# Strided and local attention before two gated products: prologue loads cut in 15/16 and 1/16 of their rows, wider query-key matmuls, small matmuls ahead

## The chip, the cores and the metric

One core of a Trainium2 chip runs the kernel. The metric is the device time of one execution in microseconds (us), as the median of several runs. Beside it one execution was taken by the hardware profiler; its rows are those quoted here. Engines are named as in the profile: PE (TensorE's matmuls), PEld (its weight loads), DVE (VectorE), ACT (ScalarE), POOL (GpSimd), SP (SyncE, which issues the transfers).

## The reference

The inputs are q, k, v of 4 batches x 8 heads x 576 positions x 64, and three weight matrices for each of two gated products on 2304 tokens of 512.

```
scores = scale * np.matmul(q, k.transpose(0, 1, 3, 2))
mask_local = (rel >= 0) & (rel < stride)                  # heads 0 to 3, stride 32
mask_strided = (rel >= 0) & (pos[None, :] % stride == pos[:, None] % stride)   # heads 4 to 7
...
attn = np.exp(scores - max);  attn = attn / (sum + 1e-09);  x = np.matmul(attn, v)
x = (x @ w_a) * (x @ w_b) @ w_out
x = sigmoid(x @ w_gate) * (x @ w_val) @ w_out
```

## The kernel before

The 576 positions are cut into tiles of 128 (the last has 64), and a tile of all four batches makes 512 tokens. The first tile is the prologue: its attention has to be done before the first gated product has anything to multiply. From there on the products of a tile run on PE while DVE and ACT do the attention of the next tile and convert the weights.

**The local heads of the first tile** are four groups, one per batch (`attention`, with `first` true). A group is a chain over the engines: load of q and k (`load_qk`) and of v for two batches at a time (`load_v`); on PE the mask by a matmul with the identity and then eight matmuls of 64 rows by 64 keys (`qk`, L605 and L611); on DVE maximum (L623); on ACT four exponentials (L629); the sum's reciprocal (L635, L636) and the normalisation (`normalise`, L644) on whichever of POOL, DVE and ACT the plan finds free first; four transposes on PE (L652), a copy on ACT (L658), the product with v on PE (L668), and two parts of the result on ACT and DVE (L677, L680), which are columns of the tiles x12 and x14. The strided heads of the same tile are `strided_first` (scores L994 and L1001, transposes L1032, values L1065, results L1082 and L1086 in x13 and x15).

**The weights** come in pieces of 512 KB (`convert`). Each is turned from its stored form on ACT (L519), DVE (L528), ACT (L536) and DVE (L540). The first three go to the buffer `raw`. The next three (`k == 1`) go to a place of their own in w4, and before each of these loads POOL copies one element from the landed first weight into that place (L512), so that the load waits for it.

**The order** on each engine is made by a planner (`Plan.run`): it keeps a time for each engine, takes the operation that can begin first, and writes the engines' streams in that order. The times are costs given with each operation, such as 450 for a load on SP or 1050 for a normalisation on POOL. Nothing of it is known to the chip: there each engine takes its stream in order and waits at semaphores. Where the planner leaves a gap on PE in the first 27 us, it fills it with matmuls by zeros (`plan.fill`, L447, and L1056 later on).

The products of the first tile with w_a and w_b are L1117, with w_out L1208; the second gated product is L1489.

Of the kernel before, what the change touches and what calls it, by code (L numbers as in the profile page):

```python
# [11 lines left out]
U16 = mybir.dt.uint16  # L12
# [45 lines left out]

IDLE_BANK, FILL_TO = 3, 27e3
FILL = (430, 8e3, 225)  # L60

M1, M2 = 400, 50

# [119 lines left out]
class Plan:  # L183
# [85 lines left out]

    def run(self):  # L270
        avail = dict.fromkeys(("PE", "ACT", "DVE", "POOL", "SP", "ACTQ"), 0.0)
        dma = 0.0
        left = {}
        after = {}
        ready = []
        for op in self.ops:
            left[op] = len(op.deps)
            for d in op.deps:
                after.setdefault(d, []).append(op)
            if not op.deps:  # L280
                ready.append(op)
        while ready:
            best = None
            for op in ready:
                s = self.start(op, avail)
                if s is None:
                    continue
                t, eng, cost, slots = s
                rank = (max(t, avail[eng]), op.key, op.seq)
                if best is None or rank < best[0]:  # L290
                    best = rank, op, eng, cost, slots
            if best is None:
                raise RuntimeError("no operation can be issued")
            rank, op, eng, cost, slots = best
            ready.remove(op)
            if eng == "PE" and self.fill and rank[0] < FILL_TO:
                t = avail["PE"]
                while True:
                    t += FILL[0] if t < FILL[1] else FILL[2]
                    if t > rank[0]:  # L300
                        break
                    self.fill()
            op.eng = eng
            op.slot = {}
            for (ring, _), (_, s) in slots.items():
                op.slot.setdefault(ring, []).append(s)
                self.held[ring, s] = op
            op.end = avail[eng] = rank[0] + cost
            if op.size:
                early = eng == "SP" and op.end < 20e3  # L310
                dma = max(dma, op.end + 700) + op.size / (330 if early else 350)

                op.end = dma + (1700 if early else 1200)
            op.fn(op)
            for ring, owner in op.free:
                if isinstance(owner, tuple):
                    held = owner[0].slot[ring][owner[1]:owner[1] + 1]
                else:
                    held = owner.slot[ring]
                for s in held:  # L320
                    del self.held[ring, s]
                    self.since[ring, s] = op.end
            for x in after.get(op, ()):
                left[x] -= 1
                if not left[x]:
                    ready.append(x)
        self.makespan = max(avail.values())
# [35 lines left out]
def attention_moe_kernel(ctx, tc, qkv, fqk, fvv, fq, fk, fv, sq, sk, sv, w1, w2, mask, ident, out):  # L363
# [77 lines left out]
    for n in range(B):  # L441
# [5 lines left out]
    plan.fill = lambda: PE.matmul(  # L447
        idle, nil, nil.unsqueeze(1).to_broadcast([P, 4, P]), start=True, stop=True)

    c_id = add("ACTQ", 600, lambda op: ACT.dma_start(out=idt, in_=ident), size=1 << 16)  # L450
    mask_at = weight(2, KF - 7, 1, EARLY)

# [31 lines left out]
    def convert(w, need, start=()):  # L484
        parts, done, merges = {}, {}, []
        tops, firsts = [], []

        def clear(op):
            for i in op.slot["c"]:
                tops.append(at(PLACE["c"] + i * DM, DM, FIRST, U32))  # L490
                POOL.memset(tops[-1], 0)

        c_top = add("POOL", 1000, clear, start, key=need(0, 0) - AHEAD - 10,
                    take=[("c", F_RING[:1]), ("c", F_RING[1:])])
        for c in range(3 * KF):
            k, m = divmod(c, 3)
            x = {}
            key = need(k, m) - AHEAD
            at_load = key - LEAD

            if k == 0 and m < 2:
                key -= EARLIER

            own = (RAW_ZONE * ZONE + m * 2 * DM, 2 * DM, EARLY) if k == 1 else None
            if k == 0:
                firsts.append(x)

            def load(op, x=x, k=k, m=m, own=own):

                x["raw"] = at(*own, U32) if own else raw(op, U32)[:, :2 * DM]  # L510
                if own:
                    POOL.tensor_copy(out=x["raw"][:1, :1], in_=firsts[m]["raw"][:1, 1:2])  # L512
                nc.sync.dma_start(
                    out=x["raw"].bitcast(U16)[:, :4 * DM - 1], in_=w[k, m].bitcast(U16)[:, 1:]
                )

            def top(op, x=x):
                x["t"] = tops[op.slot[f"t{id(w)}"][0]]
                ACT.activation(  # L519
                    out=x["t"].bitcast(F16).rearrange("p (n two) -> p n two", two=2)[:, :, 1],  # L520
                    in_=x["raw"].bitcast(BF16).rearrange("p (n four) -> p n four", four=4)[:, :, 2],
                    func=AF.Copy, scale=0.5,
                )

            def merge(op, x=x):
                u = x["raw"].rearrange("p (n two) -> p n two", two=2)[:, :, 0]
                x["f"] = u.bitcast(F32)
                DVE.scalar_tensor_tensor(  # L528
                    out=u, in0=u, scalar=13, in1=x["t"],
                    op0=ALU.logical_shift_right, op1=ALU.bitwise_or,  # L530
                )

            def high_part(op, x=x, k=k, m=m):
                hi, lo = (at(*weight(m, k, i), F32R) for i in range(2))
                parts[m, k] = hi, lo
                ACT.activation(out=hi, in_=x["f"], func=AF.Copy, scale=256.0)  # L536

            def low_part(op, x=x, k=k, m=m):
                hi, lo = parts[m, k]
                DVE.scalar_tensor_tensor(  # L540
                    out=lo, in0=x["f"], scalar=256.0, in1=r32(hi),
                    op0=ALU.mult, op1=ALU.subtract,
                )

            plan.slack = M2
            taken = [] if own else [("raw", (0, 1, 2))]
            used = [own] if own else []
            after = [firsts[m]["op"]] if own else []
            a = touch(add("SP", 450, load, list(start) + after, key=at_load, take=taken, size=1 << 19), (), used)
            x["op"] = a  # L550
            b = touch(add("ACT", act(512), top, [a, c_top], key, take=[(f"t{id(w)}", (0, 1))]), used)
            end = c == 3 * KF - 1
            f = add("DVE", dve(512), merge, [b] + merges * end, key,
                    free=[(f"t{id(w)}", b)] + [("c", c_top)] * end)
            merges.append(f)
            touch(f, (), used)
            g = touch(add("ACT", act(512), high_part, [f], key), used, [weight(m, k, 0)])
            h = touch(add("DVE", dve(512), low_part, [g], key, free=[] if own else [("raw", a)]), used, [weight(m, k, 1)])
            done[m, k] = g, h
            plan.slack = 0  # L560
        return parts, done
# [5 lines left out]
    def attention(g, key, banks, first, war, load=(), held=None, last=True):  # L567
# [13 lines left out]
        def load_qk(op):  # L581
            if first:
                a = at(*eqk)[:, :QW + KW]
                nc.sync.dma_start(out=a, in_=fqk[n])
                x["q"], x["k"] = a[:, :QW], a[:, QW:]
            else:
                a = qk_buf(op)[:, :QW + g.kw]
# [2 lines left out]

        def load_v(op):
            if first:
                nc.sync.dma_start(out=at(*evv)[:WB], in_=fvv[:, n // 2 * 2 * VW:][:, :2 * VW])
                return
            x["v"] = small(op)[:WB, :g.vw]
            nc.sync.dma_start(out=x["v"], in_=qkv[n, :WB, QW + KW:QW + KW + g.vw])
# [5 lines left out]
        def qk(op):  # L602
# [3 lines left out]
            e = at(*ee) if first else small(op)  # L606
            x["e"] = e[:, :g.width]
            for i in range(g.nb):
                for e in range(2):
                    o, k = i * WB + e * HB, g.key(i) + e * HB  # L610
                    PE.matmul(  # L611
# [79 lines left out]
        def ring(*r):  # L691
# [2 lines left out]

        qks, vs, es = ((0, 1), V_RING[:2], E_RING) if g.i != 1 else ((0,), V_RING[:1], E_RING[:1])

        lq = add("SP", 450, load_qk, load, key=FRONT_KEYS[0][n] if first else key - 10, take=ring(("qk", qks)),
                 size=P * (QW + g.kw) * 4)
        used(lq, (), [eqk])
        if first and n % 2:  # L700
            lv = pairs[n // 2]
        else:
            lv = add("SP", 450, load_v, load, key=FRONT_KEYS[1][n // 2] if first else key - 8, take=ring(("c", vs)),
                     size=WB * g.vw * 4 * (1 + first))
            used(lv, (), [evv])
            if first:
# [260 lines left out]
    def strided_first(key):  # L967
# [8 lines left out]
        qa, ka, va, ea, pa = FRONTS["strided"]  # L976

        def load(a, src, at_key):
            return touch(add("SP", 450, lambda op: nc.sync.dma_start(out=at(*a), in_=src), (), at_key,
                             size=P * a[1] * 4), (), [a])  # L980

        lq, lk, lv = (load(a, b, c) for a, b, c in zip((qa, ka, va), (fq, fk, fv), FRONT_KEYS[2]))
# [822 lines left out]
```

## Time and profile before

| | |
|---|---|
| median of 3 runs | 901.54 us (901.32 to 901.73) |
| the profiled execution | 900.82 us |
| its span, first to last instruction | 899.0 us |
| PE busy | 889.7 us (99%) |
| DVE, ACT, POOL busy | 647.4, 405.3, 3.6 us |
| mean granted PE clock | 0.998 |

The busy share of PE is near the whole span, so the time is that of PE's work and of the few places where it waits. A timeline shows for each piece the start, the duration, the engine and line, what it writes and reads, and in brackets how long the engine had been idle before it and what released it; "issue" is a wait that nothing in the profile explains. The queue called instruction in the tables of transfers brings the engines' programs; q8 moves packets of 16 KB.

### The profile page before, as it was taken

The page shows a single profiled execution, that of the slowest core. Times are in us where ns is not written, and L with a number is a line of the kernel's source. Part 1 is how long each engine was busy: PE and PEld are TensorE (multiplying, and loading weights), DVE is VectorE, ACT ScalarE, POOL GpSimd, SP SyncE. Part 2 cuts the span into 40 slices and gives each one's busy share as a digit, 9 for nine tenths or more (in the row PEclk, how much of TensorE's full clock was granted, in tenths as well). Part 3 has the DMA queues.
Part 4 walks back from the last instruction along what each step waited for, and adds up shares of the span by engine and source line. Part 5 has one row for each costly group of instructions (what it writes and reads, how often), then busy time and mean ns, then how long its engine had stood idle before and what let it go on. Part 6 is the DMA issues. An engine that isn't in the chain of part 4 may idle for free.

```text
span 899.0 us, 14095 instructions
## 1 busy us (share of the span) xinstructions
PE 889.7 (99%) x5408; PEld 801.9 (89%) x5408; DVE 647.4 (72%) x1062; ACT 405.3 (45%) x841; POOL 3.6 (0%) x15
## 2 busy tenths in 40 slices
PE   8999999999999999999999999999999999999998
PEld 4788888888888888888899999999999999999998
DVE  4999988998999779811329876674768468649491
ACT  4876644411242113311236655564656545435351
POOL 0000000000000000000000000000000000000000
PEclk9999999999999999999999999999999999999999
DMA  8676664212332123300035243645675598953501
GB/s 306 226 252 191 197 207 131 92 44 63 89 131 72 54 65 117 124 1 0 1 118 164 94 141 127 201 157 186 213 230 181 183 325 317 375 166 116 168 18 61
DMA packets 60515, 132.72 MB, mean 148 GB/s; under 512 B 5728, under 2 KB 35040, under 8 KB 59552
## 3 DMA queue, kind: packets, MB, share of 16 engines
q1 hardware_dynamic: 60160, 131.60, 44.2%
q8 instruction: 42, 0.69, 0.3%
q10 hardware_dynamic: 288, 0.23, 0.1%
q14 instruction: 25, 0.20, 0.1%
HBM read 97.20 MB, written 34.60 MB: 147 GB/s over the span
## 4 chain that ended last, share of the span: by engine, by line
PE 98%; DVE 1%; ACT 1%; issue 0%
PE bank L1489 43%; PE bank L1117 33%; PE bank L1208 17%; PE bank L668 1%; PE bank L611 1%; PE bank L652 1%; PE idle L447 1%; PE bank L938 0%; ACT w8p L629 0%; DVE w4p L1445 0%; PE bank L1065 0%; DVE rest L1501 0%; ACT w4p L1442 0%; PE bank L1056 0%; DVE rest L1572 0%
## 5 line engine op out<-in xcount | busy, mean ns | idle before, releaser
L1142 ACT CAST h16p<-rest 128x512 fp32r<-128x512 f32 (+1 forms) x60 | 34.7, 579 | 133.2 <-PE bank L1208 132.5
L1501 DVE TENSOR_TENSOR rest<-bank,rest 128x384 f32<-128x384 f32 x84 | 46.3, 554 | 57.8 <-PE bank L1489 32.4
L1138 DVE TENSOR_TENSOR rest<-bank,rest 128x512 f32<-128x512 f32 (+1 forms) x60 | 38.1, 634 | 52.0 <-PE bank L1117 51.1
L1262 ACT COPY rest<-bank 128x512 f32<-128x512 f32 (+1 forms) x60 | 32.6, 544 | 91.1 <-PE bank L1117 89.2
L1507 ACT COPY rest<-bank 128x384 f32<-128x384 f32 x84 | 40.2, 479 | 66.1 <-PE bank L1489 65.9
L1146 DVE TENSOR_TENSOR h16p<-rest,h16p 128x512 fp32r<-128x512 f32 (+1 forms) x60 | 38.1, 635 | 29.9 <-PE bank L1208 23.2
L842 DVE TENSOR_TENSOR rest<-rest 128x320 f32<-128x320 f32 (+13 forms) x56 | 51.5, 920 | 1.5 <-DMA rest<-sq 0.5
L905 DVE TENSOR_TENSOR rest<-rest,s 128x320 f32<-128x320 f32 (+13 forms) x56 | 51.5, 919 | 0.9
L912 DVE TENSOR_REDUCE rest<-rest 128x64 f32<-128x320 f32 (+13 forms) x56 | 51.2, 914 | 1.0
L848 DVE TENSOR_REDUCE s<-rest 128x5 f32<-128x320 f32 (+13 forms) x56 | 51.1, 913 | 1.0
L1399 DVE SCALAR_TENSOR_TENSOR rest<-rest 128x512 uint32<-128x512 uint32 x36 | 24.6, 687 | 11.8 <-ACT rest L1392 11.6
L1392 ACT ACTIVATE rest<-rest 128x512 f16<-128x512 bf16 x36 | 28.0, 790 | 7.4 <-DMA rest<-w 7.4
L519 ACT ACTIVATE rest<-rest 128x512 f16<-128x512 bf16 x33 | 26.2, 795 | 10.0 <-DMA rest<-w 9.7
L1572 DVE TENSOR_TENSOR rest<-bank,rest 128x384 f32<-128x384 f32 x36 | 20.0, 556 | 12.4 <-PE bank L1489 10.6
L1566 ACT ACTIVATE rest<-bank 128x384 f32<-128x384 f32 x36 | 17.6, 490 | 22.3 <-PE bank L1489 22.0
L1511 ACT COPY bank<-bank 128x384 f32<-128x384 f32 x42 | 19.5, 466 | 17.3 <-PE bank L1489 16.9
L629 ACT ACTIVATE rest<-bank,nm 128x96 f32<-128x96 f32 x56 | 18.3, 338 | 12.0 <-DVE nm L624 10.5
L528 DVE SCALAR_TENSOR_TENSOR rest<-rest 128x512 uint32<-128x512 uint32 x33 | 22.5, 684 | 0.4 <-ACT rest L519 0.2
L1566 ACT ACTIVATE rest<-rest 128x768 f32<-128x768 f32 x18 | 15.3, 848 | 13.9 <-DVE rest L1501 13.6
L1489 PE MATMUL bank<-w8p,w10p 128*128 128x384 f32 x100 | 20.7, 334 | 0.0
L1489 PEld LDWEIGHTS bank<-w8p,w10p 128*128 128x128 f32 x100 | 17.6, 188 | 0.0
L1489 PE MATMUL bank<-x15p,w3p 128*128 128x384 f32 x88 | 17.5, 334 | 0.0
(494 smaller groups left out, 2395.9 us busy)
## 6 DMA issues: line engine op xcount, KB each, us to landing
rest<-w SPq DMA_DIRECT2D x69, 511.8 KB, 4.3
h2d<-rest SPq DMA_DIRECT2D x18, 768.0 KB, 4.0
rest<-qkv SPq DMA_DIRECT2D x12, 416.0 KB, 4.3
w2p<-h2d SPq DMA_DIRECT2D x12, 384.0 KB, 5.5
w0p<-h2d SPq DMA_DIRECT2D x12, 384.0 KB, 5.2
w1p<-h2d SPq DMA_DIRECT2D x12, 384.0 KB, 5.8
out<-rest SPq DMA_DIRECT2D x24, 192.0 KB, 1.8
x2d<-rest SPq DMA_DIRECT2D x16, 256.0 KB, 2.5
```

The lines of the kernel that those rows point to most:

```text
L842: engine[op.eng].tensor_tensor(out=product(op, n), in0=x["k", h][:, :, :n, :], in1=x["q"][h // 2][:, e:e + nh, j:j + 1, :].to_broadcast([P ...
L848: DVE.tensor_reduce(out=weights_of(h, j, n), in_=x["p", op.deps[0]], op=ALU.add, axis=AX.X)
L905: engine[op.eng].tensor_tensor(out=product(op, n, "p (h d t) -> p h d t"), in0=x["v", h][:, :, :, :n], in1=weights_of(h, j, n).unsqueeze(2 ...
L912: DVE.tensor_reduce(out=xs[:, j, e:e + nh, :], in_=x["p", op.deps[0]], op=ALU.add, axis=AX.X)
L1117: PE.matmul(x[tag][:, :n], ww[:, c * P:(c + 1) * P], xx(c), start=(u == 0 and c == chunks[0]), stop=(u == last and c == chunks[-1]),)
L1138: DVE.tensor_tensor(out=x["g"], in0=x["b"][:, :n], in1=x["g"], op=ALU.mult)
L1142: ACT.copy(out=x["hh"], in_=x["g"])
L1146: DVE.tensor_tensor(out=x["hl"], in0=x["g"], in1=r32(x["hh"]), op=ALU.subtract)
L1208: PE.matmul(ps[:, :n], ww[:, m * P:(m + 1) * P], x[xx], start=start, stop=stop)
L1489: PE.matmul(bank_of(where), at(*lhs(a, (0, 1, 0)[q], c), F32R), at(*rhs(b, (0, 0, 1)[q], c), F32R), start=p in OPENS and (q, c) == units[0 ...
L1501: DVE.tensor_tensor(out=at(*o), in0=bank_of("Z"), in1=at(*a), op=ALU.add)
L1507: "ACT", act2(NS), lambda op: ACT.copy(out=at(*o), in_=bank_of("Y")), [ops[after]], key - 20))
```

## The change

There are three edits. `split_load` replaces the transfers of the prologue: the rows of each are cut in a first piece of 15/16 (120 of 128, or 90 of 96) and a second one of 1/16, which are issued one behind the other. This holds for q, k and v of the first tile, for the strided heads' q, k and v, and for the first six weight loads (`w is w1 and k < 2`). The planner's cost of these loads goes from 450 to 900. The query-key matmuls of the first tile take 128 rows by 96 keys, so that a group has four of them where it had eight; what is computed beside the masked band is masked before. Eighteen matmuls of 32 x 32 zeros stand ahead of everything on PE, at 30 each in the plan.

```diff
+PADS = 18
...
         avail = dict.fromkeys(("PE", "ACT", "DVE", "POOL", "SP", "ACTQ"), 0.0)
+        avail["PE"] = 30.0 * PADS
...
+    for _ in range(PADS):
+        PE.matmul(idle[:32, :32], nil[:32, :32], nil[:32, :32], start=True, stop=True)
+
+    def split_load(out, src):
+        n = out.shape[0] // 16 * 15
+        nc.sync.dma_start(out=out[:n], in_=src[:n])
+        nc.sync.dma_start(out=out[n:], in_=src[n:])
...
-                nc.sync.dma_start(
-                    out=x["raw"].bitcast(U16)[:, :4 * DM - 1], in_=w[k, m].bitcast(U16)[:, 1:]
+                (split_load if w is w1 and k < 2 else nc.sync.dma_start)(
+                    x["raw"].bitcast(U16)[:, :4 * DM - 1], w[k, m].bitcast(U16)[:, 1:]
                 )
...
-            a = touch(add("SP", 450, load, list(start) + after, key=at_load, take=taken, size=1 << 19), (), used)
+            a = touch(add("SP", 450 + 450 * (w is w1 and k < 2), load, list(start) + after, key=at_load, take=taken, size=1 << 19), (), used)
...
-                nc.sync.dma_start(out=a, in_=fqk[n])
+                split_load(a, fqk[n])
...
             for i in range(g.nb):
+                if first:
+                    PE.matmul(g.shaped(x["s"])[:, i // 2, i % 2], x["q"][:, i * P:(i + 1) * P],
+                              x["k"][:, g.key(i):g.key(i) + WB],
+                              start=False, stop=i == g.nb - 1, skip_group_check=True)
+                    continue
```

Since costs in the plan change, the planner writes other orders. Lines of the changed kernel are 10 to 15 higher than those of the same code before (L652 becomes L667).

**POOL**, from its first memsets on (w4p is the place of the weights with k == 1, w7p the scores of batches 2 and 3, nm_293 the sums of batch 3). Before:

```order
L491 MEMSET rest 128x512 x2
L512 COPY w4p_80<-rest 1x1 x3
L793 MEMSET s_474 128x128
L793 MEMSET s_1384 128x192
L793 MEMSET s_2028 128x256
```

And in the changed kernel:

```order
L501 MEMSET rest 128x512 x2
L522 COPY w4p_80<-rest 1x1
L659 ISA
L659 TENSOR_TENSOR w7p_83<-w7p_83,nm_293 128x384
L522 COPY w4p_80<-rest 1x1 x2
L808 MEMSET s_491 128x128
```

The normalisation of batch 3 has moved from DVE to POOL, between the first and the second of the copies that release weight loads. The instruction called ISA ahead of it is new as well: in the built program it is a reload of GpSimd's library 0, put directly ahead of the operation; the program before has none.

**PE**, at the transposes of batch 1 (bank_273 before, bank_266 now). Before:

```order
L652 MATMUL bank_238<-idt,w8p_84 96x128 x4
L605 LDWEIGHTS idb
L605 MATMUL bank_246<-mskb,idb 128x384
L611 MATMUL bank_246<-w9p_85 64x64 x8
L605 LDWEIGHTS idb
L605 MATMUL bank_258<-mskb,idb 128x384
L611 MATMUL bank_258<-w9p_85 64x64 x8
L652 MATMUL bank_273<-idt,w8p_84 96x128 x4
L447 LDWEIGHTS nil
L447 MATMUL idle<-nil 128x512
```

And in the changed kernel:

```order
L667 MATMUL bank_266<-idt,w8p_84 96x128 x4
L615 LDWEIGHTS idb
L615 MATMUL bank_274<-mskb,idb 128x384
L620 MATMUL bank_274<-w9p_85 128x96 x4
L615 LDWEIGHTS idb
L615 MATMUL bank_283<-mskb,idb 128x384
L620 MATMUL bank_283<-w9p_85 128x96 x4
L449 LDWEIGHTS nil
L449 MATMUL idle<-nil 128x512
```

The transposes of batch 1 now stand ahead of the scores of batches 2 and 3, and those of batch 0 have gone ahead of the strided scores. Counted in the built programs (an f32 matmul is four instructions, a transpose two, the others one), instruction 450 of PE is the second of the transposes of batch 1 before, and is among the first products with v (L683) now.

**PE**, at the transposes of batch 3 (bank_437 before, bank_454 now). Before:

```order
L668 MATMUL bank_424<-w7p_83,w8p_84 64x64 x8
L652 MATMUL bank_437<-idt,w7p_83 96x128 x4
L1056 LDWEIGHTS nil
L1056 MATMUL bank_381<-nil 128x256
L1056 LDWEIGHTS nil
```

And in the changed kernel:

```order
L683 MATMUL bank_442<-w7p_83,w8p_84 64x64 x8
L667 MATMUL bank_454<-idt,w7p_83 96x128 x4
L1132 MATMUL bank_462<-x13p_431,w0p_439 128x512 x2
L1071 LDWEIGHTS nil
L1071 MATMUL bank_360<-nil 128x256
L1071 LDWEIGHTS nil
L1071 MATMUL bank_360<-nil 128x256
L1132 MATMUL bank_462<-x15p_432,w0p_439 128x512
```

Ahead of these transposes the changed kernel has no filling matmul on PE; behind them stand three products with weights (L1132), then as before the product of batch 3 with v and the products that read x12.

## Rows read from the trace of the kernel before

**Rows 1.** The page: span, and busy time, share and instructions by engine.

```profile
span 899.0 us, 14095 instructions
PE 889.7 (99%) x5408; PEld 801.9 (89%) x5408; DVE 647.4 (72%) x1062; ACT 405.3 (45%) x841; POOL 3.6 (0%) x15
q8 instruction: 42, 0.69, 0.3%
```

**Rows 2.** Stretches: length, busy us (instructions) of five engines, clock, transfers' share, GB/s.

```profile
12.80:16.20 3.40, 0.71 (x17) 0.45 (x13) 3.23 (x9) 0.63 (x1) 0.00 (x0) 1.00 1.02 337
16.20:19.60 3.40, 2.79 (x8) 1.20 (x8) 0.04 (x1) 1.87 (x9) 0.35 (x2) 0.50 0.73 253
30.00:890.00 860.00, 858.82 (x4925) 780.90 (x4924) 629.67 (x1016) 388.11 (x786) 1.79 (x5) 1.00 0.44 144
```

**Rows 3.** Timeline, 9.7 to 19 us: PE and ACT around PE's gap.

```profile
9.74 1.29 PE L1001 MATMUL bank<-w11p 64*32 64x32 f32 x128
...
13.20 0.31 PE L652 MATMUL bank<-idt,w8p 128*96 128x128 f32 x1
...
16.81 0.88 PE L652 MATMUL bank<-idt,w8p 128*96 128x128 f32 x3 [3.30 <-issue]
...
17.73 0.58 ACT L658 COPY w8p<-bank 96x512 f32<-96x512 f32 x1 [3.97 <-PE bank L652]
...
18.21 0.34 ACT L629 ACTIVATE w7p<-bank,nm 128x96 f32<-128x96 f32 x1
```

**Rows 4.** Transfers in 14.5 to 16 us, by queue: packets, MB, share.

```profile
q1 hardware_dynamic: 161, 0.60, 98.6%
q8 instruction: 1, 0.02, 4.6%
```

**Rows 5.** Timeline, POOL from 0.7 us, and ACT's table load.

```profile
0.73 0.98 POOL L491 MEMSET rest<- 128x512 uint32 x2 [0.29 <-POOLq L1792]
...
1.65 1.28 ACT L458 ACT_TABLE_LOAD   x1 [1.65 <-PEq L1792]
...
17.32 0.17 POOL L512 COPY w4p<-rest 1x1 uint32<-1x1 uint32 x1 [15.61 <-DMA rest<-w]
```

**Rows 6.** Issues of one weight load at 6.22 and at 17.52 us: KB, us to landing.

```profile
rest<-w SPq DMA_DIRECT2D x1, 511.8 KB, 11.1
w4p<-w SPq DMA_DIRECT2D x1, 511.8 KB, 4.0
```

**Rows 7.** Timeline, 22.8 to 42.5 us: batch 3 from its normalisation to the products.

```profile
22.84 0.55 DVE L644 TENSOR_TENSOR w7p<-w7p,nm 128x384 f32<-128x384 f32 x1
...
24.32 0.69 PE L668 MATMUL bank<-w7p,w8p 96*64 96x64 f32 x16
...
24.93 0.64 PE L652 MATMUL bank<-idt,w7p 128*96 128x128 f32 x4
...
25.56 0.68 ACT L536 ACTIVATE w0p<-rest 128x512 fp32r<-128x512 f32 x1
...
26.13 0.59 ACT L658 COPY w7p<-bank 96x512 f32<-96x512 f32 x1
...
27.25 0.69 PE L668 MATMUL bank<-w7p,w8p 96*64 96x64 f32 x16
...
27.98 0.37 ACT L677 CAST x12p<-bank 128x256 fp32r<-128x256 f32 x1
...
28.25 1.43 ACT L519 ACTIVATE rest<-w4p 128x512 f16<-128x512 bf16 x2
...
28.44 0.70 PE L1117 MATMUL bank<-x12p,w0p 128*128 128x512 f32 x2
...
33.30 0.62 PE L1117 MATMUL bank<-x12p,w1p 128*128 128x512 f32 x2
...
39.61 2.88 PE L1208 MATMUL bank<-h16p,w0p 128*128 128x512 f32 x12
```

More of the change, by code (lines that the diff above doesn't have):

```diff
@@ L592, in load_v @@
             if first:
-                nc.sync.dma_start(out=at(*evv)[:WB], in_=fvv[:, n // 2 * 2 * VW:][:, :2 * VW])
+                split_load(at(*evv)[:WB], fvv[:, n // 2 * 2 * VW:][:, :2 * VW])
                 return
@@ L695, in attention @@
         qks, vs, es = ((0, 1), V_RING[:2], E_RING) if g.i != 1 else ((0,), V_RING[:1], E_RING[:1])
-        lq = add("SP", 450, load_qk, load, key=FRONT_KEYS[0][n] if first else key - 10, take=ring(("qk", qks)),
+        lq = add("SP", 450 + 450 * first, load_qk, load, key=FRONT_KEYS[0][n] if first else key - 10, take=ring(("qk", qks)),
                  size=P * (QW + g.kw) * 4)
@@ L702, in attention @@
         else:
-            lv = add("SP", 450, load_v, load, key=FRONT_KEYS[1][n // 2] if first else key - 8, take=ring(("c", vs)),
+            lv = add("SP", 450 + 450 * first, load_v, load, key=FRONT_KEYS[1][n // 2] if first else key - 8, take=ring(("c", vs)),
                      size=WB * g.vw * 4 * (1 + first))
@@ L978, in load @@
         def load(a, src, at_key):
-            return touch(add("SP", 450, lambda op: nc.sync.dma_start(out=at(*a), in_=src), (), at_key,
+            return touch(add("SP", 900, lambda op: split_load(at(*a), src), (), at_key,
                              size=P * a[1] * 4), (), [a])
```

## The prediction, made before the change was run

> **What bounds the kernel now.** I read the busy times first [rows 1]: PE is busy for 889.7 of 899.0 us, so only what PE does and where it waits can move the time. The stretches come next [rows 2]: from 30 to 890 us PE is idle for 860.00 - 858.82 = 1.2 us. All that the change touches lies ahead of that, in the prologue; whatever it gains or loses is the shift of the moment at which PE's unbroken work begins. So the question is what sets that moment, and I follow it in the timelines.
>
> The one large wait is at 13.5 us [rows 3]: the first of four transposes of batch 1 runs at 13.20, the other three at 16.81, after 3.30 us of "issue", a wait for nothing that the profile shows. ACT stands still for 3.97 us for these transposes, and the exponentials of batch 2 begin only behind that, at 18.21. In the middle of the gap lies a 16 KB packet of the instruction queue [rows 4]: PE waited for its own program. 42 such packets serve 10,816 instructions of PE and PEld [rows 1], one in 257, and this one had to share its transfer engine with a queue that was full (98.6% of sixteen engines' time). It took 4.6% of 16 x 1.5 us = 1.1 us itself. After the gap the clock is granted at 0.50 for 3.4 us, before and after it at 1.00 [rows 2].
>
> [...]
>
> From there the chain to PE's unbroken work goes through batch 3 [rows 7]: normalised on DVE at 22.84, transposed at 24.93, copied on ACT at 26.13 (ACT was busy with a weight until then), multiplied with v at 27.25, result on ACT at 27.98, first product that reads x12 at 28.44.
>
> **The change, part by part.** *The code wait.* If the 120-row pieces leave one transfer engine without rows, and the instruction queue uses that one, the 3.30 us go. Even if not, the place has moved: the same count of instructions now ends in the first products with v, no longer inside the transposes for which ACT waits. ACT's next work then begins about 17.73 - 14.0 = 3.7 us earlier (3.30 idle, and 0.4 that the transposes took longer at half clock: 0.88 for three against 0.64 for four [rows 3, 7]). Alone, this would bring batch 3's transposes from 24.93 to about 21.2.
>
> *The matmuls.* Four groups lose four calls each; they run beside waits of PE for loads and for ACT, so I cost them at nothing, at most 0.2 us a group, and that only if the rest of the chain lets them. *The eighteen small matmuls* stand where PE has only zeros to multiply, and cost nothing on the path; were the first masks ready earlier, under 1 us.
>
> *What is new on POOL.* Batch 3 is now normalised on POOL, and ahead of it stands a reload of GpSimd's library. POOL takes its stream in order: the first copy waits for the first weight, which was there at 17.32 [rows 5], then comes the reload, then the normalisation. PE waits for it at the transposes with nothing else to do, and ACT waits for PE at the copy behind them. So the 3.7 us have a new end:
>
> 1. The first copy. The same bytes lie ahead of it. Without the code packet it could come 1.1 us earlier, so end at 16.4; if the sixteenth row falls as a ninth row on engines that have eight, an eighth of the 13 us that the loads flow is added, 1.6 us: 19.1. I take 17.9.
> 2. The reload. No row shows one. The lowest neighbour is ACT's table load, 1.28 us [rows 5]; the highest a whole 512 KB weight through the full queues, 11.1 us [rows 6]. The nearest in kind is code for PE. With one packet in 257 instructions, I read it as asked for 257 instructions ahead of the gap, which is some 80 instructions into the strided scores that begin at 9.74 [rows 3], so at 10.1; PE went on at 16.81: 6.7 us under the same queues. I take 6.7.
> 3. The normalisation. On DVE 0.55 us [rows 7]; POOL sets 128x512 in 0.49 [rows 5]. With two operands I take twice the DVE, 1.0, bounds 0.55 and 1.6, and 0.1 for the semaphores.
>
> Transposes of batch 3: 17.9 + 6.7 + 1.1 = 25.7, against 24.93: **+0.8 us**. The bounds are 18.3, where POOL no longer sets it and the 21.2 from above does, and 31.8, +6.9.
>
> [...]
>
> 4. From transposes to products. Before: 28.44 - 24.93 = 3.51 us. Now ACT has waited and takes the copy at once: 0.64 + 0.59 + 0.69 + 0.37 + 0.15 for hand-overs = 2.45. In both orders three products that do not read x12 have run by then. **-1.0 us**, between 0 and -1.1.
> 5. The clock. PE's last work ahead of these transposes, batch 2's product with v, ended at 25.0 [rows 7] and would end at 21.3 by the 3.7 us; until 25.7 it has nothing, 4.4 us, longer than the 3.30 us behind which 0.50 was granted [rows 2]. If the same comes, the transposes and the product with v (0.64 + 0.69) take up to twice as long: **+1.1 us**, bounds 0 and 1.7 (half of a 3.4 us stretch of bound work).
>
> What queues behind POOL: the second and third copy, and with them on SP two weight loads and all loads after them. The second of these weights lands about 26 + 4.0 [rows 6] = 30, and from its first conversion to the product with w1 lay 33.30 - 28.25 = 5.1 us [rows 7], so about 35. PE needs this half of w1 only twelve products, 2.9 us [rows 7], behind the first with w1, so at 33.30 + 0.9 + 2.9 = 37: covered by 2 us, and each microsecond of reload moves both.
>
> **Sum:** 0.8 - 1.0 + 1.1 = +0.9 us on the span of 899.0. The profiled execution took 900.82 us, 0.72 below the median of the runs; carried over to the median, 901.54 + 0.9 = **902.4 us**. A measurement of this kernel can tell about 0.2%, 1.8 us, from no change, so this is "the same". Its own range, with the reload between 5 and 8 us and the clock's bounds: 899.7 to 903.3.
>
> **The rivals.** *Faster, the reload costs nearly nothing.* Point of decision: a reload under 21.2 - 1.1 - 17.9 = 2.2 us ends before batch 3 is there, and the whole 3.7 us stay: 897.8 us. The table load of 1.28 us speaks for it, and that the library may be there already; against it, that code comes by transfer and the one case in this trace waited long. Between 2.2 and 5 us part of it stays.
>
> *Slower, the reload meets the full queues.* At 17.9 two weights are still coming in and a third goes out. If the reload waits like a load there, 9 to 11 us, the transposes come at 28 to 30, and with a half clock over the start the time is 904.7 to 907; it decides from about 8 us up (+1.3 more than I took, and the clock in full). [...]
>
> *The change doesn't do what it says:* the instruction queue's engine carries rows all the same. Then PE stops at the products with v at about 15 to 18, but as long as POOL holds batch 3 beyond 24 this hides behind it: 902 again; with a quick reload about 901.
>
> **How the numbers follow.** The forecast 0.40 together with the third rival's 902; the fast reload 0.23; the slow one 0.32; beyond 907, if the loads behind POOL come too late as well, 0.05. Range: from the fast case to the slow one with their bounds, 897.6 to 906.4, leaving out under 0.1 on each side. Faster by over 0.2%: 0.25; within: 0.39; slower: 0.36.
>
> **What would show it.** In the changed profile the 3.30 us "issue" at the transposes of batch 1 should be gone and ACT's copy there at about 14; the instruction packet should come within 2 us of being needed. POOL's normalisation should start about 6.7 us after its first copy, and PE's largest wait should be at L667 for POOL, from about 21.3 to 25.7, with half clock behind it. If POOL's two rows lie within 2 us of each other, the fast rival holds; if over 8 us, the slow one. A second long wait of PE in 28 to 45 us for weights would show that the loads behind POOL were not covered, and a stop at L683 that the code wait stays.

## The result, and the profile after

The changed kernel takes **908.88 us** (median of 4 runs, 908.41 to 909.98) beside 901.63 us (901.32 to 902.57) for the kernel before on the same chip: a ratio of 1.008, with a 95% interval of 1.0063 to 1.0098. It is slower by 7.25 us, and 2.5 us above the upper end of the range. The profiled execution took 908.8 us.

The page of the changed kernel, for [rows 1]; the two added lines are PE's clock in tenths and the chain that ended last:

```profile
span 907.0 us, 14098 instructions
PE 894.7 (99%) x5396; PEld 806.6 (89%) x5396; DVE 647.9 (71%) x1061; ACT 405.5 (45%) x841; POOL 4.4 (0%) x16
PEclk9799999999999999999999999999999999999999
q8 instruction: 42, 0.69, 0.3%
PE 96%; DMA 2%; DVE 0%; issue 0%; ACT 0%; SPq 0%
```

The span is longer by 8.0 us, and the chain now holds 2% of transfers, three loads of 19.9 us together, of which the kernel before had none. The chain of waits of the changed kernel in order of time (start, length, what) says where:

```profile
0.73 4.70 DMA idt<-ident
5.81 6.98 DMA w11p<-fk
12.81 8.20 DMA w9p<-fvv
21.46 1.16 PE bank L683 x29
...
26.91 2.23 issue
29.13 1.29 PE bank L1080 x41
30.43 1.05 PE bank L683 x16
31.48 1.02 PE bank L667 x4
```

Until 21 us the end is set by three loads, the identity, the strided keys and the values; then by PE's work, much of it at half clock (granted 0.50 from 32 to 36 us), and in it a wait of 2.23 us. The rate of the transfers shows why the loads set it. Stretches of both kernels (length, busy us of five engines, clock, transfers' share, GB/s), first before, then after:

```profile
8.00:12.00 4.00, 4.00 (x159) 2.71 (x155) 2.78 (x11) 3.04 (x17) 0.00 (x0) 1.00 1.04 384
```

```profile
8.00:12.00 4.00, 3.25 (x21) 1.91 (x20) 2.61 (x10) 3.21 (x17) 0.00 (x0) 1.00 0.97 220
16.00:20.00 4.00, 2.50 (x15) 1.46 (x14) 2.60 (x10) 2.78 (x16) 0.00 (x0) 1.00 0.96 216
20.00:24.00 4.00, 2.84 (x39) 2.59 (x40) 1.65 (x6) 0.98 (x4) 0.00 (x0) 0.79 0.97 229
24.00:28.00 4.00, 2.85 (x92) 1.78 (x91) 2.52 (x7) 2.57 (x5) 1.16 (x3) 0.78 0.96 237
28.00:32.00 4.00, 2.87 (x60) 2.67 (x60) 1.50 (x4) 1.12 (x4) 0.31 (x2) 0.65 0.95 225
32.00:36.00 4.00, 4.00 (x28) 2.51 (x27) 2.34 (x4) 2.54 (x5) 0.00 (x0) 0.50 1.02 236
```

The sixteen transfer engines are as busy as before (0.95 to 1.02 of their time), yet they move 216 to 237 GB/s where they moved 384. It is the single packet that takes longer: among the trace's packets from 4 to 20 us, the median one of 4096 bytes takes 159 ns before (from loads of 128 rows) and 281 ns after, one of 3328 bytes 131 and 227 ns. POOL's first copy, which reads the first weight, answers [rows 5], and behind it comes the new normalisation:

```profile
25.05 0.17 POOL L522 COPY w4p<-rest 1x1 uint32<-1x1 uint32 x1 [23.33 <-DVE x14p L695]
25.26 0.81 POOL L659 TENSOR_TENSOR w7p<-w7p,nm 128x384 f32<-128x384 f32 x1
27.38 0.17 POOL L522 COPY w4p<-rest 1x1 uint32<-1x1 uint32 x1 [1.31 <-DMA rest<-w]
```

The first copy comes at 25.05 us in the place of 17.32; the normalisation follows 0.21 us behind it, 0.04 us after its end. The profile puts the copy's wait down to DVE's L695; that ended at the same moment by chance, since in e1 below, with the same order, the copy runs at 17.46 us and L695 at 22.03. And PE, for [rows 3] and [rows 7]:

```profile
17.76 1.46 PE L449 MATMUL idle<-nil 128*128 128x512 bf16 x6
21.14 1.47 PE L683 MATMUL bank<-w8p,w9p 96*64 96x64 f32 x32 [1.93 <-DMA w9p<-fvv]
22.55 1.12 PE L1047 MATMUL bank<-idt,w10p 128*128 128x128 f32 x4
23.45 1.06 PE L667 MATMUL bank<-idt,w7p 128*96 128x128 f32 x4
24.31 1.06 PE L449 MATMUL idle<-nil 128*128 128x512 bf16 x2
25.43 1.48 PE L1080 MATMUL bank<-w10p,w11p 32*64 32x32 f32 x87
29.13 1.29 PE L1080 MATMUL bank<-w10p,w11p 32*64 32x32 f32 x41 [2.23 <-issue]
30.36 1.12 PE L683 MATMUL bank<-w7p,w8p 96*64 96x64 f32 x16
31.41 1.09 PE L667 MATMUL bank<-idt,w7p 128*96 128x128 f32 x4
...
36.39 0.71 PE L1132 MATMUL bank<-x12p,w0p 128*128 128x512 f32 x2
```

The same work in the kernel before, from the products with the values on:

```profile
19.70 1.15 PE L668 MATMUL bank<-w8p,w9p 96*64 96x64 f32 x32
20.78 0.66 PE L1032 MATMUL bank<-idt,w10p 128*128 128x128 f32 x4
21.87 0.61 PE L652 MATMUL bank<-idt,w7p 128*96 128x128 f32 x4
22.43 1.96 PE L1065 MATMUL bank<-w10p,w11p 32*64 32x32 f32 x128
```

The first product that reads x12 has gone from 28.44 [rows 7] to 36.39 us, by 7.95, which is nearly the whole 8.0 us of the span. It comes in three parts. The products with the values start 1.44 us later (21.14 against 19.70). From there to batch 3's transposes it was 5.23 us and is 10.27: 2.23 for the wait inside L1080, nearly all the rest for rows that take up to twice as long, in stretches with a granted clock of 0.79 to 0.50 behind PE's waits (1.12 us against 0.66 for the strided transposes, 1.06 against 0.61 for batch 2's). POOL is not on this path: its normalisation ended at 26.07 us, and PE came to the transposes that need it at 31.41. From the transposes to the product it was 3.51 and is 4.98, at half clock too.

### The profile page after: what moved, and what is told of

Read it like the earlier page. It is cut to its first block, busy times and chain, and to the rows that moved or that the text cites. A ratio compares the mean times of both kernels' runs of the same rounds, so it can differ in the third digit from the quotient of the medians.

```text
span 907.0 us, 14098 instructions
## 1 busy us (share of the span) xinstructions
PE 894.7 (99%) x5396; PEld 806.6 (89%) x5396; DVE 647.9 (71%) x1061; ACT 405.5 (45%) x841; POOL 4.4 (0%) x16
## 4 chain that ended last, share of the span: by engine, by line
PE 96%; DMA 2%; DVE 0%; issue 0%; ACT 0%; SPq 0%
PE bank L1504 43%; PE bank L1132 33%; PE bank L1223 16%; PE bank L683 1%; DMA w9p<-fvv 1%; PE bank L667 1%; PE bank L626 1%; DMA w11p<-fk 1%; DMA idt<-ident 1%; PE bank L953 0%; PE bank L1080 0%; PE bank L1071 0%; DVE w4p L1460 0%; DVE rest L1516 0%; ACT w4p L1457 0%
```

## The experiments

Every time is a median, and its ratio is to runs of the kernel before on the same chip (901.63 us for the changed kernel, 902.70 to 903.05 for the others); across rows of different chips the ratios are to be compared, not the times. "First x12" is the start of the first product that reads x12, 28.44 in the profile before, and GB/s is that of 8 to 12 us. Both come from one execution each, and the one of the kernel before, at 900.82 us, was 2 us below the medians of that kernel beside e1 to e13, so that differences of 1 or 2 us in "first x12" against it prove nothing.

| run | what it is | us | ratio to before, 95% | GB/s | first x12 |
|---|---|---|---|---|---|
| after | the change | 908.88 | 1.0063 to 1.0098 | 220 | 36.39 |
| e1 | the change with whole loads | 906.12 | 1.0027 to 1.0052 | 396 | 33.32 |
| e2 | before with cut loads | 911.03 | 1.0074 to 1.0101 | 222 | 34.06 |
| e3 | the change, 64 and 64 rows | 909.05 | 1.0053 to 1.0079 | 241 | 36.23 |
| e4 | the change, 112 and 16 rows | 904.20 | 1.0006 to 1.0025 | 293 | 31.30 |
| e5 | the change, halves by columns | 904.05 | 1.0004 to 1.0025 | 398 | 32.56 |
| e6 | before, 18 matmuls by zeros | 903.82 | 1.0002 to 1.0020 | 398 | 30.81 |
| e7 | before, wide matmuls | 905.07 | 1.0013 to 1.0031 | 389 | 32.41 |
| e8 | before, both of these | 905.22 | 1.0018 to 1.0039 | 398 | 32.47 |
| e9 | before, 5 fillers fewer | 902.34 | 0.9989 to 1.0006 | 393 | 29.81 |
| e10 | wide, 32 matmuls by zeros | 903.39 | 0.9997 to 1.0015 | 388 | 31.05 |
| e11 | wide, 29 matmuls by zeros | 902.55 | 0.9992 to 1.0010 | 384 | 29.82 |
| e12 | wide, three small loads | 902.86 | 0.9989 to 1.0008 | 400 | 29.08 |
| e13 | wide, 13 fillers fewer | 905.60 | 1.0017 to 1.0040 | 390 | 31.21 |

### What slows the loads: e1 to e5

The theory after the first look: pieces with fewer rows move at a lower rate, and the rest follows. The rivals: the new order of instructions costs the time, or the number of transfers does.

**e1_whole**

```diff
     def split_load(out, src):
-        n = out.shape[0] // 16 * 15
-        nc.sync.dma_start(out=out[:n], in_=src[:n])
-        nc.sync.dma_start(out=out[n:], in_=src[n:])
+        nc.sync.dma_start(out=out, in_=src)
```

> The changed kernel with each load of the prologue in one piece again; its order of instructions (POOL's normalise of the pair's batch 1, the changed costs of SP), wide query-key matmuls and 18 matmuls by zeros stay. Theory 'pieces' (pieces of 120 and 8 rows, 90 and 6 rows, halve the rate of the transfers, and the rest follows from it): 216 to 240 GB/s in the prologue rises to 400 or more, POOL's first copy goes from 25.05 us back to 17 to 18 us, and the time is 898 to 903 us. Rival 'order' (the new order of instructions with POOL's normalise is what costs): the time stays at 907 to 910 us, though the loads may land early.

```profile
17.46 0.17 POOL L522 COPY w4p<-rest 1x1 uint32<-1x1 uint32 x1 [15.75 <-DMA rest<-w]
26.04 1.07 PE L1080 MATMUL bank<-w10p,w11p 32*64 32x32 f32 x38 [2.33 <-issue]
```

The rate is back (396 GB/s), the first copy stands at 17.46 us, but the time is 906.12: the loads' share came back, and 3.2 us stayed. Both theories missed the time.

**e2_split_alone**: the kernel before with `split_load` for its loads, planner's costs and all else as before.

> The kernel before with the loads of the prologue cut in 15/16 and 1/16 of their rows, nothing else: order of instructions, costs and matmuls are those of before. 'Pieces': 216 to 240 GB/s until the loads have landed, POOL's first copy at 24 to 26 us, 906 to 910 us. 'Order': 900.5 to 903 us. If both have a part, the time lies between, and e1 and e2 add up to the whole of 7.25 us.

911.03 us, first copy at 25.36, 222 GB/s: the cut alone costs 8.1 us, as much as the whole change or more (the intervals overlap), and 1 us above what was expected. PE waits 2.21 us for the strided keys (until 12.55) and 3.58 us for code at the last query-key matmul (until 21.18), and in the profiled execution two later waits come on top, of 2.31 us at the first product with w1 (until 41.42, for a copy on ACT that stood behind the conversion of a late weight) and of 1.60 us at 466.40, which none of the other profiles has at this place and which isn't shown to be the cut's. So the parts don't add up: e1 and e2 make 3.2 + 8.1 = 11.3 us in the place of 7.25. Cutting costs 8.1 us on the kernel before, and 908.88/901.63 - 906.12/902.94 = 0.45%, 4 us, on the rest of the change.

**e3_half**, **e4_7_8** and **e5_columns** keep the changed order and the count of transfers, and cut elsewhere:

```diff
-        n = out.shape[0] // 16 * 15
+        n = out.shape[0] // 2        # e3
+        n = out.shape[0] // 8 * 7    # e4
```

```diff
-        n = out.shape[0] // 16 * 15
-        nc.sync.dma_start(out=out[:n], in_=src[:n])
-        nc.sync.dma_start(out=out[n:], in_=src[n:])
+        n = out.shape[1] // 2        # e5
+        nc.sync.dma_start(out=out[:, :n], in_=src[:, :n])
+        nc.sync.dma_start(out=out[:, n:], in_=src[:, n:])
```

> The changed kernel with its loads cut in half (64 and 64 rows, 48 and 48) in the place of 15/16 and 1/16: as many transfers, the same order on every engine, the same semaphores and waits of SP. 'Pieces' in the form 'it is the row counts 120, 90, 8 and 6': as e1, 898 to 904 us, first copy at 17 to 19.5 us. Rival 'count' (twice the transfers on 8 DMA semaphores, so SP waits for landings before it issues): as the changed kernel, 906 to 910 us, first copy at 24 us or later.

> The changed kernel with its loads cut as 7/8 and 1/8 (112 and 16 rows, 84 and 12): nearly as unequal as 15/16 and 1/16, as many transfers, the same order. 'It is the row counts 120 and 8, which don't spread over 16 DMA engines': the 128-row loads are fast again (both pieces are multiples of 16 rows) and only the two 96-row loads slow, 898 to 904 us, first copy at 17 to 20 us. Rival 'small second pieces are what clogs' or 'count': 905 to 910 us, first copy at 23 us or later.

> The changed kernel with its loads cut in two halves of their columns (128 rows by half of the columns each, 96 rows for the values) in the place of rows: as many transfers, the same order and waits of SP, only each piece has all rows again. Theory 'rows' (what slows the loads is that a piece covers fewer than 128 rows; e3 with 64 rows and e4 with 112 showed it too): 370 GB/s or more from 4 to 16 us, less about a tenth for the smaller packets, first copy at 17.4 to 19 us, time as e1: 905 to 907.5 us. Rival 'count' (16 more transfers on the queue's semaphores): 240 to 290 GB/s, first copy at 21 us or later, 906 to 910 us.

The same stretch of e3, e4 and e5:

```profile
8.00:12.00 4.00, 3.35 (x61) 1.96 (x60) 2.44 (x8) 3.02 (x16) 0.00 (x0) 1.00 1.03 241
```

```profile
8.00:12.00 4.00, 3.35 (x87) 2.07 (x88) 2.58 (x9) 3.27 (x17) 0.00 (x0) 1.00 1.03 293
```

```profile
8.00:12.00 4.00, 3.35 (x35) 2.07 (x41) 2.71 (x10) 2.89 (x17) 0.00 (x0) 1.00 1.05 398
```

With as many transfers and the same waits of SP, halves by columns keep the full rate (398 GB/s beside e1's 396), halves by rows lose 40% of it (241). "Count" falls by e5. The time of e5, 904.05, is below the 905 to 907.5 that was expected (the tenth that smaller packets were to cost, an estimate of mine that rests on no row, did not show in its 398 GB/s), and e4, with slower loads than e1, is faster than e1 as well: the wait at L1080 is 0.42 us in e4 and 1.15 in e5 where e1's is 2.33, of which more below. The row of e4:

```profile
24.57 1.30 PE L1080 MATMUL bank<-w10p,w11p 32*64 32x32 f32 x41 [0.42 <-issue]
```

My special form of the theory, that it is the counts 120 and 8 which don't spread over sixteen engines, falls by e3 and e4: 64 and 112 rows are multiples of 16, and both are slow, 64 nearly as slow as 120 (first copies at 23.55 and 21.36 us). What is left is that loads of pieces which cover fewer than all 128 rows run slower: 293 GB/s with 112 and 16 rows, 241 with 64 and 64, 220 with 120 and 8, beside 398 with all 128 rows in halves by columns. Why 120 rows, at 220 GB/s, are no faster than 64, no row explains: it stays open.

The profile of the kernel before showed it already. Its values are loads of 96 rows, and the rate of its transfers in 40 slices of 4 to 20 us is:

```profile
GB/s 399 410 417 440 420 430 399 440 398 408 416 400 399 403 423 410 410 410 328 246 266 246 256 246 266 287 420 389 389 420 389 420 430 409 164 61 154 72 246 399
```

From 11.6 to 14.4 us, seven slices of 0.4 us at 246 to 287 GB/s between others at 389 and more: about 0.73 MB, nearly the two loads of 384 KB by 96 rows, which stand at this place in the queue. Their packets of 4096 bytes take 260 ns (the median from 12.0 to 13.6 us), those of 128 rows 159.

### What the other 3 us are: e6 to e13

The theory: PE stops for code at fixed counts of its instructions. Counted in the built program, the 450th stood in batch 1's transposes; 18 matmuls by zeros and their weight loads push everything back by 36, and the wide matmuls take 64 away until there. The rivals: the wide matmuls as such, or the planner's new order.

**e6_pads** is the kernel before with the loop of 18 matmuls (`PADS = 18`) and no cost for them in the plan, **e7_wide** with the four matmuls of 128 by 96 in the place of eight, **e8_pads_wide** with both.

> The kernel before with the 18 matmuls by zeros at the start of PE, nothing else; order and loads of before. They are 36 instructions more ahead of everything on PE. Theory 'code position' (the wait of 3.30 us is for code and stands at a fixed count of PE's instructions, about the 450th): it moves 36 instructions ahead, from the transposes of batch 1 to the third group of query-key matmuls, PE stops there from about 12.6 us to 16.8 us, and the time is 902 to 904.5 us. Rival (the matmuls by zeros take the wait away): PE's gap of 3.30 us is gone, 898 to 900.5 us.

> The kernel before with the wide query-key matmuls (128 rows by 96 keys), nothing else. They are 64 PE instructions fewer ahead of the products with the values. 'Code position': the wait moves behind the transposes of batch 1, into the products with the values (L683), which start later than the code lands; no gap of over 1 us between 10 and 17 us; what the wide matmuls cost is 0.35 us for each of the two later batches; 899 to 902 us. Rival 'wide matmuls cost' (e1's 3.2 us are theirs): 904 to 907 us.

> The kernel before with both, the matmuls by zeros and the wide query-key matmuls, whole loads and the order of before. It differs from e1 in the order of instructions alone (the changed costs in the planner). Theory 'order costs the 3.2 us of e1': 900 to 903 us. Rival 'code position or wide matmuls cost them': 905 to 907 us, with two waits of PE for code (at L683 and L1080) as in e1.

The timelines of PE, of e6 and of e7, around their stops:

```profile
12.34 0.69 PE L626 MATMUL bank<-w9p 128*64 128x64 f32 x16
18.10 0.48 PE L615 MATMUL bank<-mskb,idb 128*128 128x384 bf16 x1 [5.08 <-issue]
```

```profile
16.14 0.91 PE L683 MATMUL bank<-w8p,w9p 96*64 96x64 f32 x23
18.86 0.46 PE L683 MATMUL bank<-w8p,w9p 96*64 96x64 f32 x9 [1.80 <-issue]
...
20.73 1.67 PE L1080 MATMUL bank<-w10p,w11p 32*64 32x32 f32 x108
26.27 0.85 PE L1080 MATMUL bank<-w10p,w11p 32*64 32x32 f32 x20 [3.87 <-issue]
```

In e6 the stop stands 36 instructions ahead of its old place, right behind the third query-key group, at the mask of the fourth, about as said, and is longer than said, since its packet came later. In e7 it has moved into L683, behind the 23rd of 32 matmuls, which is instruction 450 (403 ahead of them and two each). Both times the packet of the instruction queue ended 1.2 us before PE went on (at 16.90 and 17.62), as in the kernel before (15.62, PE at 16.81). But a second stop has come up in L1080, behind the 108th of its 128 matmuls: 490 + 216 = 706 instructions, about 256 further, and again 1.28 us behind the end of a packet. By its trace, the expected gain of e7 (899 to 902) was lost to that stop and to the half clock behind it (0.54 from 24 to 28 us). e8 is as slow as e7 with the order of before, and e1 adds 0.1% to it in the changed order, with intervals that overlap: the order costs little or nothing.

**e9_five_fewer**, **e10_wide_32** and **e11_wide_29** move the 450th instruction on purpose:

```diff
+    skips = [None] * 5               # e9, on the kernel before
-    plan.fill = lambda: PE.matmul(
+    plan.fill = lambda: skips.pop() if skips else PE.matmul(
```

```diff
+PADS = 32                            # e10, on e7; 29 in e11
```

> The kernel before with five of its filling matmuls by zeros left out at the start of PE (10 instructions fewer), nothing else. 'Code position' (PE stops for code ahead of its 450th instruction, and ahead of every 256th after that): the stop no longer falls into batch 1's transposes but into the filling matmuls behind them; the transposes run at about 13.2 us, the products with the values may start when the code is there, at 16.8 to 17.5 us in the place of 19.70 us, and the time falls by 1 to 2.5 us: 900.5 to 902 us beside 903. Rival (the stop follows the transposes, or the start loses as much for want of fillers): no change, 902.5 to 904 us.

> The kernel before with the wide query-key matmuls and 32 matmuls by zeros ahead (64 instructions, as many as the wide matmuls save until batch 1's transposes), so that from there on every instruction of PE stands at the same count as before. 'Code position': one stop, at batch 1's transposes until about 17 us as before, none of over 1 us at L1080; 903 to 904.5 us, the wide matmuls costing 0.7 us. Rival 'the wide matmuls as such bring the stop at L1080': a gap of 2 us or more there, 905 us or more.

> As e10, with 29 matmuls by zeros (58 instructions), which puts the 450th instruction on the filling matmuls behind batch 1's transposes. 'Code position': like e9, the transposes run before the stop, the products with the values start at 16.8 to 18 us, and the time is 1 to 2 us under e10: 901.5 to 903 us. Rival: as e10 or slower.

PE of e10, and of e11:

```profile
14.81 0.27 PE L667 MATMUL bank<-idt,w8p 128*96 128x128 f32 x1
19.36 0.53 PE L667 MATMUL bank<-idt,w8p 128*96 128x128 f32 x3 [4.28 <-issue]
```

```profile
14.28 0.60 PE L667 MATMUL bank<-idt,w8p 128*96 128x128 f32 x4
18.47 2.18 PE L449 MATMUL idle<-nil 128*128 128x512 bf16 x5 [3.58 <-issue]
20.57 1.81 PE L683 MATMUL bank<-w8p,w9p 96*64 96x64 f32 x32
```

With the counts of before (e10) the stop is back inside batch 1's transposes, behind the first of four, L1080 runs through, and the time is 903.39: the wide matmuls cost 0.7 us, which these runs can't tell from nothing, and the other 1.3 us of e7's 2.0 (0.22% less 0.06%, with intervals that just overlap) are the place of the stops. In e9 and e11 the stop stands in the filling matmuls behind the transposes, as said, but the gain expected of it (1 to 2.5 us) did not come in e9: 902.34 beside 902.71, no difference. The rival had named one reason, the start loses for want of fillers: e9's first two groups of scores took 1.12 and 1.02 us where the kernel before took 0.69, and batch 1's transposes ran at 14.90, not at 13.2. The packet came later too (it ended at 17.50 us in e9 and 17.04 in e11, against 15.62 before), so that PE went on at 18.92 and 18.47 us, and then half clock lay on five fillers ahead of the products in e11 (2.18 us) and on the products in e9 (1.82 us against 1.15; granted 0.59 from 20 to 24 us in e9, 0.74 in e11). e11 lies 0.8 us below e10, less than these runs can tell apart.

**e12_small_loads** asks why the second block comes late:

```diff
-                    x["raw"].bitcast(U16)[:, :4 * DM - 1], w[k, m].bitcast(U16)[:, 1:]
+                    x["raw"].bitcast(U16)[:, :64 if own else 4 * DM - 1], w[k, m].bitcast(U16)[:, 1:65 if own else 4 * DM]
```

> e7 (wide matmuls alone) with the three weight loads behind POOL's copies cut from 2047 to 64 columns, the rest of these tiles being zeros: its products with these weights are not the reference's. Theory 'the second code block waits behind the weight loads' (in e7 its transfer starts 5.2 us after PE entered the block before it, in the kernel before 1.3 us): with 16 KB in the place of 512 KB for each of these loads it starts within 2 us of the entry, the stop of 3.87 us at L1080 shrinks to under 1.2 us, and the time falls by 2 us or more under e7's 905. Rival (the code comes late for a reason of its own): the stop stays over 3 us.

```profile
20.19 1.72 PE L1080 MATMUL bank<-w10p,w11p 32*64 32x32 f32 x108
23.54 0.54 PE L1080 MATMUL bank<-w10p,w11p 32*64 32x32 f32 x20 [1.63 <-issue]
```

The block starts to move 2.9 us after PE went on behind the first stop (e7: 5.2), the stop falls from 3.87 to 1.63 us and the time by 0.23%, 2.1 us. That is most of what the theory wanted, not all: it had said within 2 us and under 1.2. The weight loads are 2.3 of the 5.2 us of delay; 2.9 us remain with transfers at 0.07 of their time from 20 to 24 us, so a full queue is not the only reason why code comes late.

**e13_wide_13_fewer**: e7 with 13 fillers left out (`skips = [None] * 13`).

> The kernel before with the wide query-key matmuls and 13 filling matmuls by zeros fewer at the start: 64 and 26 instructions fewer, so that PE's 450th instruction is the filling matmul ahead of batch 2's transposes, which in e7 ran at 19.74 us. Theory 'the second block is asked for when PE enters the block before it, and its delay of 1.2 to 5.7 us is mostly loads ahead of it': the first block (asked for as early as in e7, landed by 17.6 us) is there in time, so no stop before 19.7 us; PE enters it at about 19.7 us, the last of the weight loads is issued at 21.3 us, and the second stop, at the 706th instruction, has shrunk to under 2.5 us; 901 to 904 us. Rival 'the second block comes 5 us or more after the entry whatever is ahead of it' : a stop of 2.5 to 4 us at L1080, 904 to 906 us. That PE has nothing to do before 5 us may cost clock; the granted clock of 8 to 20 us shows it.

There is no first stop, and the second is 2.10 us (23.84 to 25.94), both as the theory said: the block began to move 2.9 us after PE came to the fillers at 20.84, 2.3 after it left them. The time, 905.60, lies in the rival's range (904 to 906), for other reasons: PE had nothing until 5.54 us, its first query-key groups took 1.86 us each where e7's took 1.03, and the strided scores began at 13.70 in the place of 10.78. The granted clock, which was to show this, reads 1.00 from 8 to 12 us; only the lengths of the matmuls show it. In the profiled execution a wait of 1.49 us at 747 us, for a copy on ACT, comes on top; first x12 itself, at 31.21, is ahead of e7's 32.41. None of these kernels is faster than the one before.

**What stays open:** what the second block's delay hangs on besides loads. From PE's entry into the block ahead to the first byte it was 1.2 us in e10 and 1.3 in the kernel before, 2.0 to 2.9 in e9, e11, e12 and e13, 3.5 to 4.1 in e1, e4, e5 and e6, 5.0 and 5.2 in e8 and e7, and over 5 in the changed kernel, e2 and e3, with their slow loads. And how the 4 us that the cut adds to e1 divide into late values, the stop and half clock was read from the trace of the changed kernel, and not tried apart.

## Why the prediction was wrong, step by step

*Where the time is decided* was right: the shift of the first product with x12 is nearly the whole shift in span for the changed kernel (7.95 of 8.0) and for e1 (4.88 of 4.9); e2 and e13 have later waits as well.

*POOL's sum, part 1, the first copy*, is the step that failed. I took 17.9 us and at most 19.1, from "the same bytes lie ahead of it" and one eighth for a ninth row. It came at 25.05 and ended at 25.22. That the bytes move at the same rate was not read anywhere; the nearest rows for a load of fewer rows were the two of 96 rows in the kernel before, at 246 to 287 GB/s. At 266 in the place of 400 the 13 us of loads take 19.5, which would have put the copy near 24. The rows were looked at by landing time and not by rate. No rival had slow loads in it; with whole loads (e1, 0.4% slower) the time would have been about 905 us on this chip, an estimate, and inside the range; the cut's 4 us put it outside.

*The path* failed with it. The sum lets late loads act through POOL alone, with PE waiting for POOL at batch 3's transposes. POOL was done at 26.07 us, against 25.7 in the sum with its hand-over, but that is luck: the first copy ended 7.3 us late and the reload was 6.7 us short. And PE did not wait for POOL: it came to those transposes at 31.41 us, held up by the load of the values (products with them from 21.14), by the stop of 2.23 us for code in L1080, and by the half clock.

*Part 2, the reload*, was off by as much to the other side: 6.7 us were taken, 0.04 us lay between copy and normalisation (whether that library was there already, no run shows). The fast rival was right in this. It gave 897.8 on the ground that 3.7 us would then stay; e1, where loads and normalisation are both quick (first copy at 17.46 us, normalisation 0.83 us), shows that they don't (906.12). *Part 3, the normalisation,* was 0.81 us, within 0.55 to 1.6.

*The code wait.* Where it would go was right, and the third rival named it: e1 and e4 stop inside the products with the values at L683 (1.80 and 1.32 us); in the changed kernel itself the values landed at the same time, so that the profile puts the wait down to them. That the transposes no longer wait was right too: ACT's copy came at 14.72 (about 14 expected).

```profile
14.72 0.58 ACT L673 COPY w8p<-bank 96x512 f32<-96x512 f32 x1 [2.56 <-PE bank L667]
```

That the short pieces might spare an engine for the code did not show: the 16 KB packet took 1.21 us (18.73 to 19.94) where it took 1.10 before. What I left out is the next block, 256 instructions on. With the first stop behind the transposes PE runs into L1080, whose 256 instructions take 1.96 us without a stop (e10), before the next packet has come: 2.23 us in the changed kernel, 2.33 in e1, 3.87 in e7. The gain of 3.7 us at the transposes was given back there and in the half clock behind it (0.65 from 28 to 32 us and 0.50 from 32 to 36 in the changed kernel).

*The wide matmuls* at nothing: 128x96 took 275 ns where 128x64 took 222, and a group 1.03 to 1.10 us where it took 0.69, so they are dearer by 0.4 us a group, not cheaper; on the path that is 0.7 us (e10), which can't be told from nothing. *The eighteen small ones* cost nothing themselves, but as 36 instructions they move the stops (e6: 5.08 us in the place of 3.30, the time +0.1%).

*From transposes to products* was -1.0 us by the sum and +1.47 in the trace, at a clock of 0.50. *The half clock* I had at +1.1 us for three rows; it lay on part of PE's work from 21 us on (clock 0.79, 0.78 and 0.65 in the stretches from 20 to 32) and on all of it from 32 to 36 (0.50). And one bound of the sum was added up wrongly: a reload of 8 us with the clock in full makes 902.4 + 1.3 + 0.6 = 904.3, not 903.3; the stated range does not hang on it.

## What to carry to other kernels

If a load has to be cut, cut it by columns and not by rows: here the loads in pieces of fewer than 128 rows moved at 0.55 to 0.75 of the rate (220 to 293 GB/s), and halves by columns at the full rate (398). Cutting gained nothing in either form. Before a load's shape is changed, look in the trace for a load that already has the new shape, and read its GB/s. And where PE runs many short matmuls early, count instructions: here those that were added or taken away moved the stops for code by as many, and a stop that was moved off one chain opened the next one. And when a sum comes out near the measured row, check that the row lies on the path: POOL's did not.

## What the runs showed of the hardware that was not expected

- The rate by rows of a piece, with all sixteen engines' time full (0.97 to 1.05 from 8 to 12 us): 384 to 398 GB/s with 128 rows, 293 with 112 and 16, 241 with 64 and 64, 220 with 120 and 8, 246 to 287 with 96. The packet of 4096 bytes takes 159 ns with 128 rows, 260 with 96 and 281 with 120 and 8.
- PE's stops for code stood at instruction 450 or 706, give or take one, in each kernel in which they were counted (before, after, e6 to e8, e10, e11, e13), and PE went on 1.2 to 1.4 us after the packet's end. The stops were 1.40 to 5.08 us long in e6, e7 and e12, the last of e12, of 1.63 us, with transfers at 0.07 of their time from 20 to 24 us.
- The instruction ahead of POOL's normalisation, in the built program a reload of GpSimd's library, left no time between POOL's rows: 0.04 us, from 25.22 to 25.26. At 25.2 us the trace has two instructions MODIFY_POOL_CONFIG of 1 ns of this line.
